# One stage's instruction order and weight loads, and the queues of stores and gates, in a three-part transformer block

## The chip, the cores and the metric

The kernel runs on one core of a Trainium2 chip. The core has a matrix engine (TensorE, PE in the profile, with its weight load as PEld), VectorE (DVE), ScalarE (ACT), GpSimd (POOL) and SyncE (SP); each runs its own instructions in order, and semaphores join them. SP and POOL issue the transfers here. The metric is the device time of one execution in microseconds (us), the median of several.

## The reference, cut to what matters

```python
def reference(q, k, v, g_norm, moe_*, moe2_*):       # q, k, v: [8, 8, 576, 64]
    kv = einsum('bhsd,bhse->bhde', k, v)
    o = einsum('bhsd,bhde->bhse', q, kv)
    x = (o / rms(o) * g_norm) as [4608, 512]          # attention without softmax
    expert = argmax(norm(x) @ norm(expert_emb).T / tau)   # 8 experts, top 1
    x = gate * (relu(x @ w1[expert]) @ w2[expert])    # 512 -> 1024 -> 512
    h = x @ w_in                                      # 512 -> 2048
    return (h * cos(h)) @ w_out                       # 2048 -> 512
```

All data are float32, but `w_in` and `w_out`, which come as 64-bit numbers.

## The kernel before

It has three stages. Products are made to float32 precision out of three matmuls each: every operand is split into a high part (a copy by ScalarE into the matmul's format) and a low part (the difference, by VectorE), and high x high, high x low and low x high are added in PSUM (`PASS`, L229).

**Attention** (0 to about 185 us): the products with k, v and q, the norm, the logits, and a scatter of the tokens to their experts' rows.

**Experts** (about 185 to 625 us): 16 chunks of 304 tokens, in turns `g` of one eighth of a chunk (130 turns). A turn runs `layer1` and, two turns later, `layer2` of a slice, splits a piece of expert weights that SP loaded some three turns earlier (`load_piece`, L125, `split_piece`), and does a slice of the next chunk's gate (`gate_x`, L161). A gate is stored to and loaded back from a small table (L207 to 212), by POOL for chunks 1 to 10, else by SP (`BY_POOL`, L74); the same constant says who stores a chunk's `perm` rows and its result in `yT` (`store_y`, L259). Beside this the weights of the last stage are converted: from turn 16 on (`2 * OPEN`, L1097) two or three times a turn the generator `conv` is advanced, which reads 64-bit weights by POOL, rounds them on VectorE, forms Strassen-like sums of the blocks and stores seven 256 KB units for each eighth of `w_in` (`ws`) and of `w_out` (`wo`) by POOL (`prepare`, L411, L438). The tile `WAB[0]` that these stores read is later the ring of streamed weights.

**Last stage** (from about 625 us): nine blocks of 512 tokens (`NB`), each in eight steps of 256 hidden columns: 72 steps `i`, then two more for what lags. Both matrix products use the Winograd form of Strassen's method: seven products in place of eight. Step `i` does three things at once. TensorE makes the seven hidden products of step `i` ("h" units, named A11, S1, S2, S4, S3, A12, A22 after their weights) and the six or seven output products of step `i - 2` ("o" units a11, a22, s2, a12, s3, s1, and on odd steps `t`, two units long); `units` (L448) gives their order. A unit has six matmuls of 128x128 by 256 columns. VectorE and ScalarE finish the hidden values of step `i` (two halves, `h1` and `h0`: the sums of the products, then turns of the angle, `parts`, the cosine, and the product with it) and form sums and high and low parts of step `i - 1`.

The hidden products go to two PSUM banks, `ha` and `hb`, one buffer each. Each is read before the next unit may write it: `one` (ScalarE copies `ha` after A11), `five` (copies `hb` after S1), `two` (copies `ha` after S2), then VectorE adds `two` and `hb` (`h1`, first half), `five` and `ha` (`h1`, second half), `one` and `hb` (`h0`, first half), and ScalarE copies `ha` (`h0`, second half). A next step's A11 needs that last copy. `t` is put into `hb` too. The order on each engine is the order of the text in `step` (L1265): the cosine of the half left from the step before and its product on VectorE come first (L1293), then `one` (L1316), the sums, `five`, the highs; at the end come turns, `parts` of the second half (L1380 to 1382). The next block's tokens are split by `tokens_of` (L344), a generator that is advanced once after each step (L1404).

SP loads weights in the order of use into a ring of `RS` = 9 slots of 256 KB (`slot`, `feed`, L461 to 474): each unit that used a slot calls `feed` for the unit nine further. Of the output weights, four units of each eighth are kept in SBUF (`KEPT`, 32 quarters of 256 KB): `keep` loads four of them at a time, for two eighths ahead of step 0 and for one ahead of each of steps 1 to 6 (L1389 to 1392). The final sums of a block stand at the start of the second step after it (`after`), behind sums in the step before that (`done`); POOL scatters the rows out.

## Time and profile before

| | us |
|---|---|
| median of 3 runs | 1478.63 (1478.52 to 1481.57) |
| the profiled execution | 1477.85 |
| its span, first to last instruction | 1476.4 |
| attention stage | 0 to 185 |
| experts stage | 185 to 624.7 |
| last stage, steps 0 to 7 | 624.7 to 720.4 |
| last stage, steps 8 to 71 | 720.4 to 1450.7 |
| rest | 1450.7 to 1476.4 |

Durations and starts come from the profiled execution; the median is that of other executions, 0.8 us apart here. A matmul's end is modelled, and matmuls overlap, so the distance of two starts tells more than a duration. The lists of waits name the engine and line that waited, and what ended the wait.

### The profile page before, as it was taken

The page shows a single profiled execution, that of the slowest core. Times are in us where ns is not written, and L with a number is a line of the kernel's source. Part 1 is how long each engine was busy: PE and PEld are TensorE (multiplying, and loading weights), DVE is VectorE, ACT ScalarE, POOL GpSimd, SP SyncE. Part 2 cuts the span into 40 slices and gives each one's busy share as a digit, 9 for nine tenths or more (in the row PEclk, how much of TensorE's full clock was granted, in tenths as well). Part 3 has the DMA queues.
Part 4 walks back from the last instruction along what each step waited for, and adds up shares of the span by engine and source line. Part 5 has one row for each costly group of instructions (what it writes and reads, how often), then busy time and mean ns, then how long its engine had stood idle before and what let it go on. Part 6 is the DMA issues. An engine that isn't in the chain of part 4 may idle for free. (4 is left out here: it accounts for less than half of the span.)

```text
span 1476.4 us, 30084 instructions
## 1 busy us (share of the span) xinstructions
PE 1343.0 (91%) x10825; PEld 1302.5 (88%) x10825; DVE 1124.5 (76%) x2551; ACT 780.8 (53%) x1601; POOL 229.6 (16%) x407
## 2 busy tenths in 40 slices
PE   7997999999999999978998989989899898998995
PEld 6876999899999999968988989889898898988995
DVE  2568869988988987557777878778687787777875
ACT  4567355554555454345555555555555555555552
POOL 1242323333433331000010100101001010010101
PEclk9999999999999999989999999999999999999998
DMA  9998587977988874499777878778677787886782
GB/s 267 307 314 251 179 208 233 287 240 238 265 255 231 265 250 127 131 331 329 244 273 226 272 239 259 265 231 281 221 260 263 228 278 229 254 275 220 254 263 100
DMA packets 233795, 363.28 MB, mean 246 GB/s; under 512 B 26604, under 2 KB 113424, under 8 KB 232424
## 3 DMA queue, kind: packets, MB, share of 16 engines
q1 hardware_dynamic: 209368, 277.20, 60.3%
q0 software_dynamic: 24256, 84.06, 17.6%
q8 instruction: 89, 1.46, 0.4%
q14 instruction: 66, 0.54, 0.1%
q10 hardware_dynamic: 16, 0.02, 0.0%
HBM read 302.24 MB, written 58.96 MB: 245 GB/s over the span
## 5 line engine op out<-in xcount | busy, mean ns | idle before, releaser
L254 PE MATMUL y<-h,ring 128*128 128x304 f32 x1536 | 237.6, 304 | 13.6 <-DVE yo L262 12.9
L237 PE MATMUL hps<-xT,ring 128*128 128x304 f32 x1536 | 244.6, 309 | 3.1 <-DVE xT L226 2.9
L254 PEld LDWEIGHTS y<-h,ring 128*128 128x128 f32 x1536 | 221.4, 189 | 15.9 <-issue 12.8
L237 PEld LDWEIGHTS hps<-xT,ring 128*128 128x128 f32 x1536 | 222.4, 191 | 5.4 <-DVE xT L226 4.3
L1162 ACT ACTIVATE u<-u,half_pi 128x512 f32<-128x512 f32 x144 | 103.6, 720 | 157.6 <-DVE u L1159 157.6
L1253 POOL DMA_INDIRECT out<-o_sb,perm_i x36 | 39.1, 1086 | 857.8 <-DVE o_sb L1226 518.6
L1245 DVE TENSOR_TENSOR h<-h,u 128x512 f32<-128x512 f32 x144 | 99.3, 690 | 85.5 <-ACT u L1162 84.7
L1156 ACT ACTIVATE u<-h 128x512 int32<-128x512 f32 x144 | 91.0, 632 | 133.1 <-DVE lo L1229 129.6
L1186 PE MATMUL ha<-ring,wa 128*128 128x256 f32 x738 | 115.7, 294 | 24.8 <-ACT one L1223 17.7
L1186 PEld LDWEIGHTS ha<-ring,wa 128*128 128x128 f32 x738 | 99.0, 196 | 32.3 <-ACT one L1223 23.6
L1196 PE MATMUL o_a<-ring,hi 128*128 128x256 f32 x640 | 122.8, 284 | 0.0
L1159 DVE SCALAR_TENSOR_TENSOR u<-h,u 128x512 f32<-128x512 f32 x144 | 98.8, 686 | 23.6 <-ACT u L1156 23.6
L1186 PE MATMUL ha<-xb,wa 128*128 128x256 f32 x600 | 92.6, 290 | 24.9 <-ACT one L1223 21.2
L1186 PEld LDWEIGHTS ha<-xb,wa 128*128 128x128 f32 x600 | 79.0, 191 | 31.8 <-ACT one L1223 26.9
L1196 PEld LDWEIGHTS o_a<-ring,hi 128*128 128x128 f32 x640 | 99.5, 192 | 0.0
L1229 DVE TENSOR_TENSOR lo<-u,hi 128x512 fp32r<-128x512 f32 x144 | 98.4, 684 | 0.0
L141 DVE TENSOR_TENSOR ring<-raw,ring 128x1024 fp32r<-128x1024 f32 x72 | 87.7, 1218 | 12.5 <-ACT ring L140 12.3
L1196 PE MATMUL o_s<-wa,hi 128*128 128x256 f32 x456 | 86.9, 282 | 4.8 <-DMA wa<-wo 4.8
L1196 PE MATMUL o_a<-ring,lo 128*128 128x256 f32 x320 | 90.3, 282 | 0.6 <-DVE lo L1229 0.6
L1223 ACT ACTIVATE hi<-u 128x512 fp32r<-128x512 f32 x144 | 88.7, 628 | 3.5 <-DVE u L1229 0.2
L243 ACT ACTIVATE h<-hps 128x304 fp32r<-128x304 f32 x128 | 53.2, 416 | 70.1 <-PE hps L237 68.7
L244 DVE SCALAR_TENSOR_TENSOR h<-hps,h 128x304 fp32r<-128x304 f32 x128 | 59.7, 466 | 35.4 <-ACT h L243 35.1
(271 smaller groups left out, 3083.7 us busy)
## 6 DMA issues: line engine op xcount, KB each, us to landing
wa<-ws SPq DMA_DIRECT2D x390, 256.0 KB
wa<-wo SPq DMA_DIRECT2D x170, 256.0 KB
raw<-in_moe_w SPq DMA_DIRECT2D x144, 256.0 KB
ring<-ws SPq DMA_DIRECT2D x114, 256.0 KB
ring<-wo SPq DMA_DIRECT2D x78, 256.0 KB
ws<-wa POOLq DMA_DIRECT2D x56, 256.0 KB, 5.3
wo<-wa POOLq DMA_DIRECT2D x56, 256.0 KB, 4.9
xr<-xs POOLq DMA_DIRECT2D x16, 627.0 KB, 7.6
```

The costliest lines, as they stand in the source:

```text
L141: nc.vector.tensor_tensor(out=w[:, 1], in0=raw, in1=w[:, 0].bitcast(F32), op=ALU.subtract)
L237: nc.tensor.matmul(out=p[:, 0:CH], lhsT=w[:, a, k * 128:(k + 1) * 128], rhs=c["xT"][b_][k], start=(n == 0), stop=(n == 11),)
L244: V.scalar_tensor_tensor(out=lo, in0=p[:, 0:CH], scalar=0.0, in1=hi.bitcast(F32), op0=ALU.max, op1=ALU.subtract)
L254: nc.tensor.matmul(out=c["y"][d][:, 0:CH], lhsT=w[:, a, 512 + d * 128:512 + (d + 1) * 128], rhs=h[b_], start=(f == 0 and i == 0), stop=(f ...
L1156: nc.scalar.activation(out=n, in_=p, func=ACTF.Copy, scale=TURN, bias=0.25)
L1159: V.scalar_tensor_tensor(out=u, in0=p, scalar=TURN, in1=n, op0=ALU.mult, op1=ALU.subtract)
L1162: nc.scalar.activation(out=u, in_=u, func=ACTF.Sin, scale=2 * math.pi, bias=half_pi)
L1186: nc.tensor.matmul(out=out, lhsT=w[:, a, k * 128:(k + 1) * 128], rhs=x[xi][:, b_, k * 256:(k + 1) * 256], start=(start and n == 0), stop=( ...
L1196: nc.tensor.matmul(out=o[:, th * 256:th * 256 + 256], lhsT=G[j, name][a][:, th * 128:th * 128 + 128], rhs=w[:, b_, 0:256], start=(start an ...
L1223: nc.scalar.activation(out=out, in_=in_, func=ACTF.Copy)
L1229: V.tensor_tensor(out=out, in0=x, in1=y, op=ALU.subtract)
L1245: V.tensor_tensor(out=Y[j, t], in0=Y[j, t], in1=Y["u", t], op=ALU.mult)
```

## The change

- In `step`, ScalarE's `one` and `five` come ahead of the cosine of the half left over, with its `parts` now first on VectorE (they stood last in the step before); the sums and highs are dealt out anew between the reads of the banks; `h0`'s first add and `parts` come ahead of the last low. `t` moves ahead of `s3`. Sums of a finished block move to the step's end.
- `tokens_of` yields about twice as often, and is advanced twice inside a step: after the first high part (ScalarE's halves) and after `one` (VectorE's sums and lows).
- Kept weights: the first four quarters have a tile of their own and are loaded before the stage; the other 28 are loaded singly, one behind every second feed, at most for the next eighth but one.
- `prepare` hands the stores of `wo` to a list; SP issues one or more of them each turn, and seven ahead of the next use of their tile.
- `BY_POOL` falls from 11 to 3: gates, rows and results of chunks 3 to 10 go by SP.
- The conversion starts at turn 9 and is advanced once in a turn that splits a piece (before turn 40), else twice, three times in some.

```diff
@@ -71,7 +71,7 @@
     EARLY, EARLY_T = 2, 24
-    BY_POOL = 11
+    BY_POOL = 3
     VISITS = [(0, [0]), (1, [0, 1]), (0, [1])] + [(e, [0, 1]) for e in range(2, E)]
@@ -382,31 +380,45 @@
-        yield
+        for _ in range(4 if b else 0):
+            yield
         t1 = minus(b12, raw[0])
+        yield
         half(3, t1)
         half(0, raw[0])
-        yield
+        if b:
+            yield
         t6 = minus(raw[2], b12)
         lows()
+        yield
         half(6, t6)
-        yield
+        if b:
+            yield
         t2 = minus(raw[2], t1)
         lows()
+        yield
         half(4, t2)
         half(2, raw[2])
-        yield
+        if b:
+            yield
         t5 = minus(raw[1], t2)
         lows()
+        yield
         half(5, t5)
         half(1, raw[1])
-        yield
+        if b:
+            yield
         lows()
...
-    WA, WAB, WOUT = {}, [], {}
+    WAB, WOUT, stores = [], {}, []
+
+    def store_some(n):
+        for _ in range(min(n, len(stores))):
+            o, x = stores.pop(0)
+            nc.sync.dma_start(out=o, in_=x)
@@ -430,12 +442,16 @@
         t = WAB[0]
+        store_some(7)
         for i, n, src in ((0, 2, a[:, 0:512]), (2, 2, a[:, 512:1024]), (4, 3, o)):
...
         for u in range(7):
-            nc.gpsimd.dma_start(out=store[u], in_=t[:, u].rearrange("p a c -> p (a c)").bitcast(F32))
+            if layer:
+                stores.append((store[u], t[:, u].rearrange("p a c -> p (a c)").bitcast(F32)))
+            else:
+                nc.gpsimd.dma_start(out=store[u], in_=t[:, u].rearrange("p a c -> p (a c)").bitcast(F32))
@@ -451,7 +467,7 @@
             h(A11, B11), h(S1, T1), o("a11", W11), h(S2, T2), h(S4, B22), o("a22", W4), h(S3, T3), o("s2", V2),
-            h(A12, B21), o("a12", W21), h(A22, T4), o("s3", V3), *last, o("s1", V1),
+            h(A12, B21), o("a12", W21), h(A22, T4), *last, o("s3", V3), o("s1", V1),
         ]
@@ -472,13 +488,20 @@
         fed[0] += 1
-
-    def keep(q_):
-        WOUT[q_] = ring(WO[q_])
-        for j, w in enumerate(KEPT):
-            nc.sync.dma_start(
-                out=WOUT[q_][:, :, j * 256:j * 256 + 256].bitcast(F32), in_=wo[q_, w].rearrange("p (a c) -> p a c", a=2)
-            )
+        if fed[0] > RS and fed[0] % 2 and keeping and keeping[0][0] <= STREAM[fed[0] - RS][1] + 1:
+            keep_one()
+
+    keeping = [(q_, j) for q_ in range(8) for j in range(len(KEPT))]
+
+    def keep_one():
+        q_, j = keeping.pop(0)
+        if j == 0:
+            WOUT[q_] = ring(WO[q_ - 1]) if q_ else first_kept[0]
+        nc.sync.dma_start(
+            out=WOUT[q_][:, :, j * 256:j * 256 + 256].bitcast(F32), in_=wo[q_, KEPT[j]].rearrange("p (a c) -> p a c", a=2)
+        )
+
+    first_kept = []
@@ -1074,10 +1097,12 @@
                 cvctx.close()
-                if RS > 9:
-                    WAB.append(ctx.enter_context(tc.tile_pool(name="wb", bufs=1)).tile([128, RS - 9, 2, 256], F32R, name="wb"))
+                store_some(7)
+                first_kept.append(ctx.enter_context(tc.tile_pool(name="wb", bufs=1)).tile([128, 2, 1024], F32R, name="wb"))
                 for _ in range(RS):
                     feed()
+                for _ in KEPT:
+                    keep_one()
             if g < OPEN:
@@ -1094,8 +1119,9 @@
                 late.sort(key=lambda x: x[0])
-            if g >= 2 * OPEN:
-                for _ in range(3 if g % 4 == 0 and not splits else 2):
+            store_some(1 + len(stores) // 5)
+            if g >= START:
+                for _ in range(1 if splits and g < 5 * OPEN else 3 if g > 6 * OPEN and g % 6 == 0 and not splits else 2):
                     next(conv, None)
@@ -1282,16 +1308,16 @@
-            if after:
-                prior = b - 1
-                o1, o2 = OUT[prior]
-                add(o2[:, :, 256:512], halves(E1), halves(bank[prior, "s1"]))
-                add(o1[:, :, 256:512], halves(U2), halves(bank[prior, "s1"]))
-                out_rows(prior, 0, o1)
-                out_rows(prior, 1, o2)
+            if new:
+                xa = ps_h.tile([128, 512], F32, name="ha", tag="ha")[:, 0:256]
+                xb = ps_h.tile([128, 512], F32, name="hb", tag="hb")[:, 0:256]
+                h1, h0 = (hp_.tile([128, 512], F32, name="h", tag="h") for _ in range(2))
+                Y[i, 1], Y[i, 0] = h1, h0
+                one, five, two = (sn.tile([128, 256], F32, name=nm, tag=nm) for nm in ("one", "five", "two"))
+            else:
+                xa = xb = None
             if prev:
-                cos_of(last, 0)
-                mul_of(last, 0)
+                parts_of(last, 0)
                 r0, r1, s13, s24 = (two_of(x) for x in (Y.pop((last, 0)), Y.pop((last, 1)), Y["u", 1], Y["u", 0]))
@@ -1302,30 +1328,30 @@
                 G[last, "a22"] = (hi1[:, 0], lo1[:, 0])
-            xa = xb = None
-            if new:
-                xa = ps_h.tile([128, 512], F32, name="ha", tag="ha")[:, 0:256]
-                xb = ps_h.tile([128, 512], F32, name="hb", tag="hb")[:, 0:256]
-                h1, h0 = (hp_.tile([128, 512], F32, name="h", tag="h") for _ in range(2))
-                Y[i, 1], Y[i, 0] = h1, h0
-                one, five, two = (sn.tile([128, 256], F32, name=nm, tag=nm) for nm in ("one", "five", "two"))
+                copy(hi1[:, 0], r1[:, 1])
+                add(s13[:, 0], r1[:, 0], r1[:, 1])
+                sub(lo1[:, 0], r1[:, 1], f32(hi1[:, 0]))
+            pump()
             h(xa, True)
...
                 copy(one, xa)
-            if prev:
-                add(s13[:, 0], r1[:, 0], r1[:, 1])
-                sub(s13[:, 1], r0[:, 0], r1[:, 0])
-                sub(s24[:, 0], s13[:, 0], r0[:, 0])
-                sub(s24[:, 1], r0[:, 1], s24[:, 0])
+            if after:
+                prior = b - 1
+                o1, o2 = OUT[prior]
+                add(o2[:, :, 256:512], halves(E1), halves(bank[prior, "s1"]))
+                add(o1[:, :, 256:512], halves(U2), halves(bank[prior, "s1"]))
+                out_rows(prior, 0, o1)
+                out_rows(prior, 1, o2)
+            pump()
             if new:
...
             if prev:
-                copy(hi1[:, 0], r1[:, 1])
-                copy(hi0, r0)
-            if done:
-                copy(E1, bank[b, "a11"])
+                cosine(Y["u", 0])
+                V.tensor_tensor(out=r0, in0=r0, in1=two_of(Y["u", 0]), op=ALU.mult)
+                sub(s13[:, 1], r0[:, 0], r1[:, 0])
+                sub(s24[:, 0], s13[:, 0], r0[:, 0])
             h(xa, False)
@@ -1333,38 +1359,39 @@
             if prev:
+                sub(s24[:, 1], r0[:, 1], s24[:, 0])
+                copy(hi0, r0)
                 copy(hi13, s13)
                 copy(hi24, s24)
-                sub(lo1[:, 0], r1[:, 1], f32(hi1[:, 0]))
                 sub(lo0, r0, f32(hi0))
+            if done:
+                copy(E1, bank[b, "a11"])
             h(xa, False)
             o()
+            if prev:
+                sub(lo13, s13, f32(hi13))
             if new:
                 add(h1[:, 256:512], five, xa)
+                turns_of(i, 1)
             if done:
                 add(U2, E1, bank[b, "s2"])
-            if prev:
-                sub(lo13, s13, f32(hi13))
             if new:
...
             o()
+            if new:
+                add(h0[:, 0:256], one, xb)
+                parts_of(i, 1)
             if done:
...
                 add(OUT[b][0][:, :, 0:256], halves(E1), halves(bank[b, "a12"]))
-            if new:
-                turns_of(i, 1)
-                add(h0[:, 0:256], one, xb)
             if prev:
                 sub(lo24, s24, f32(hi24))
+            if new:
+                cos_of(i, 1)
+                mul_of(i, 1)
             h(xa, False)
-            o()
-            if done:
-                add(E1, U2, bank[b, "s3"])
-                add(OUT[b][1][:, :, 0:256], halves(E1), halves(bank[b, "a22"]))
             if new:
-                parts_of(i, 1)
-                cos_of(i, 1)
                 copy(h0[:, 256:512], xa)
@@ -1373,23 +1400,26 @@
                     add(Y["acc"], Y["acc"], t)
-                if done:
-                    add(U2, U2, Y["acc"])
             o()
+            o()
+            if done:
+                add(E1, U2, bank[b, "s3"])
+                add(OUT[b][1][:, :, 0:256], halves(E1), halves(bank[b, "a22"]))
+                add(U2, U2, Y["acc"])
             if new:
                 turns_of(i, 0)
-                mul_of(i, 1)
-                parts_of(i, 0)
             assert not todo
...
         scr = lambda: sx.tile([128, 512], F32, name="sx", tag="sx")
-        coming = None
+        coming = iter(())
+
+        def pump():
+            next(coming, None)
+
         for i in range(NS + 3):
             b, q_ = divmod(i, 8)
-            if i == 0:
-                keep(0)
-            if i < 7:
-                keep(i + 1)
+            if q_ == 0 and b + 1 < NB:
+                coming = tokens_of(b + 1, scr)
             if i < NS + 2:
@@ -1398,10 +1428,6 @@
                 out_rows(NB - 1, 1, o2)
-            if q_ == 0 and b + 1 < NB:
-                coming = tokens_of(b + 1, scr)
-            if coming:
-                next(coming, None)
             for x in range(2 * i, min(2 * i + 2, NB)):
```

Left out here: `OPEN, START = 8, 9`, the yields of `tokens_of` ahead of its first difference, and `slot` without its second tile.

## Rows read from the trace of the kernel before

**Rows 1.** The page: its first line.

```profile
span 1476.4 us, 30084 instructions
```

**Rows 2.** Table of stretches: us, busy (instructions) of each engine; PEclk, DMA, GB/s.

```profile
185.00:624.69 439.69, 422.22 (x3068) 416.82 (x3067) 370.98 (x876) 218.04 (x427) 133.70 (x251) 0.99 0.77 228
624.69:720.40 95.71, 78.83 (x591) 76.93 (x590) 62.64 (x126) 48.65 (x99) 0.00 (x0) 0.93 0.91 307
720.40:1450.67 730.27, 673.41 (x5378) 655.01 (x5377) 567.07 (x1118) 406.89 (x833) 35.16 (x32) 0.99 0.77 252
```

**Rows 3.** Waits of PE from 624 us on: total us, times, longest.

```profile
PE ha L1186 <- ACT one L1223: 50.2, 39, 1.8
...
PE ha L1186 <- DMA ring<-ws: 4.1, 1, 4.1
```

**Rows 4.** Timeline of step 22, from 880.12: start us, us, instruction, idle time before.

```profile
880.12 0.88 PE L1186 MATMUL ha<-ring,wa 128*128 128x256 f32 x6
...
880.84 0.88 PE L1186 MATMUL hb<-ring,wa 128*128 128x256 f32 x6
...
882.14 0.63 ACT L377 ACTIVATE xb<-sx 128x512 fp32r<-128x512 f32 x1 [2.80 <-DVE sx L371]
...
883.20 0.71 ACT L1162 ACTIVATE u<-u,half_pi 128x512 f32<-128x512 f32 x1
883.81 0.36 ACT L1223 ACTIVATE one<-ha 128x256 f32<-128x256 f32 x1
...
884.22 0.97 PE L1186 MATMUL ha<-ring,ring 128*128 128x256 f32 x6 [1.79 <-ACT one L1223]
```

**Rows 5.** Timeline of the stage's first step, units A11 and S1.

```profile
624.69 0.87 PE L1186 MATMUL ha<-ring,ring 128*128 128x256 f32 x6
625.40 0.88 PE L1186 MATMUL hb<-ring,ring 128*128 128x256 f32 x6
625.60 0.39 ACT L1223 ACTIVATE one<-ha 128x256 f32<-128x256 f32 x1 [4.55 <-PE ha L1186]
```

**Rows 6.** Table of stretches: steps 19 and 20, and steps 16 to 23.

```profile
845.48:856.56 11.08, 11.07 (x91) 10.87 (x91) 7.83 (x16) 6.33 (x14) 0.00 (x0) 1.00 1.01 371
856.56:867.91 11.35, 9.61 (x81) 9.32 (x79) 7.65 (x16) 6.90 (x16) 0.00 (x0) 1.00 0.60 183
...
812.46:904.22 91.76, 83.22 (x674) 80.85 (x673) 71.67 (x142) 51.34 (x105) 4.30 (x4) 1.00 0.77 252
```

**Rows 7.** Groups of ScalarE, 720 to 1450: busy us, mean ns | idle before.

```profile
L1162 ACT ACTIVATE u<-u,half_pi 128x512 f32<-128x512 f32 x128 | 92.1, 720 | 142.8 <-DVE u L1159 142.8
```

**Rows 8.** Timeline of VectorE from 906.73: the product with the cosine, two differences.

```profile
906.73 0.68 DVE L1245 TENSOR_TENSOR h<-h,u 128x512 f32<-128x512 f32 x1
907.33 0.42 DVE L1226 TENSOR_TENSOR u<-h 128x256 f32<-128x256 f32 x1
907.66 0.42 DVE L1229 TENSOR_TENSOR u<-h 128x256 f32<-128x256 f32 x1
```

**Rows 9.** Table of stretches: one at half clock, and step 1.

```profile
952.35:955.76 3.41, 3.41 (x18) 3.41 (x17) 2.15 (x6) 1.52 (x4) 0.00 (x0) 0.50 0.57 151
...
631.41:644.49 13.08, 7.02 (x43) 6.64 (x43) 7.42 (x16) 5.79 (x13) 0.00 (x0) 0.87 1.01 353
```

**Rows 10.** Waits of the experts stage, 185 to 625: us, times, longest (SPq: SP's queue).

```profile
POOL wo L438 <- DVE wa L341: 46.7, 12, 13.6
POOL gates L208 <- DVE gt L201: 29.9, 6, 12.1
...
DVE yo L262 <- DMA gate<-gates: 4.0, 2, 2.3
DVE start L487 <- POOL starti L486: 2.1, 1, 2.1
...
PE y L254 <- DVE yo L262: 12.9, 8, 3.1
...
SPq L208 <- DVE gt L201: 52.2, 5, 20.4
```

More of the change, by code (lines that the diff above doesn't have):

```diff
@@ L92, in tile_kernel @@
     NC = len(chunks)
-    OPEN = 8
+    OPEN, START = 8, 9
     use, at = [], 0
@@ L365, in tokens_of @@
         yield
-        if b > 1:
-            yield
         def minus(x, y):
@@ L383, in lows @@
             later.clear()
+        for _ in range(4 if b else 0):
+            yield
+        t1 = minus(b12, raw[0])
         yield
-        t1 = minus(b12, raw[0])
         half(3, t1)
         half(0, raw[0])
-        yield
+        if b:
+            yield
         t6 = minus(raw[2], b12)
         lows()
+        yield
         half(6, t6)
-        yield
+        if b:
+            yield
         t2 = minus(raw[2], t1)
         lows()
+        yield
         half(4, t2)
         half(2, raw[2])
-        yield
+        if b:
+            yield
         t5 = minus(raw[1], t2)
         lows()
+        yield
         half(5, t5)
         half(1, raw[1])
-        yield
+        if b:
+            yield
         lows()
@@ L464, in slot @@
             return XAT[3][:, n, 512:1024].rearrange("p (a c) -> p a c", a=2)
-        return WAB[0][:, n - 2] if n < 9 else WAB[1][:, n - 9]
+        return WAB[0][:, n - 2]
     def feed():
```

## The prediction

> **What bounds the kernel now.** The profiled execution has a span of 1476.4 us [rows 1] and a time of 1477.85, 0.8 under the median 1478.63. I first cut the span into its stages with the table of stretches [rows 2], then asked in the longest stage who makes TensorE wait [rows 3], then laid one step of it out in time [rows 4]. The reader should see this in turn. The first 72 steps of the last stage (from 624.69 on) take 826 us. From step 8 to 72 it has 730.27 us, 5378 matmul records, TensorE's mean clock at 0.99, VectorE 567 us busy and ScalarE 407 [rows 2]: no engine but TensorE is near full, yet TensorE waits. What it waits for is nearly one thing: the copy `one` on ScalarE, 50.2 us in 39 waits [rows 3]. A wait counts from the modelled end of the matmul before, so the loss is larger than that sum; I take it from starts.
>
> A unit of six matmuls starts 0.72 us after the one before (880.12 to 880.84 [rows 4]) or 0.71 (624.69 to 625.40 [rows 5]): I take 0.716. An even step has 13 units (7 hidden, 6 out), an odd one 15 (the `t` product is two more): 9.31 and 10.74 us, 80.2 for eight steps. The block at 812.46 took 91.76; its odd step of 11.08 shows that the floor is within reach, the even one of 11.35 loses 2 us [rows 6]. Steps 8 to 72 have a floor of 8 x 80.2 = 641.6, so 88.7 of 730.3 us are lost there.
>
> The reason stands in the step at 880.12 [rows 4]. In the stage's first step `one` starts 0.9 us after its unit did, 0.2 after the next [rows 5]; that is when a bank can be read. Here ScalarE, which runs in order, has token halves (from 882.14) and the cosine of the step before (883.20) ahead of `one`; `one` starts at 883.81, and the unit S2, due at 882.27, starts at 884.22. The cosine is itself late: over steps 8 to 72 ScalarE waits 142.8 us ahead of it, all for VectorE's `parts` [rows 7].
>
> **The last stage, by parts.** (1) `one` and `five` go ahead of the cosine, `parts` of the half before goes to the step's first place on VectorE, and the add that frees `hb` goes ahead of three lows. I lay a step in this order on each engine with durations from rows: 0.68 for 512 columns on VectorE (the next starts 0.60 later), 0.42 for 256 (0.33 later) [rows 8], 0.72 a cosine [rows 7], 0.36 a short copy, 0.63 a long one [rows 4]. Times count from the step's first matmul. ScalarE: `one` 0.95 to 1.32, `five` 1.66 to 2.03, cosine to 2.7, `two` 3.1 to 3.5, three highs with their waits to 5.65, turns 6.6 to 7.2, second cosine 8.0 to 8.7, last copy to 8.95. VectorE: parts to 0.69, one add, one low, token work if any to 2.6, product with the cosine to 3.4, differences, the add that frees `hb` by 4.64, two lows, the add that frees `ha` by 6.5, the next by 7.1, parts to 7.9, low, product to 9.4. TensorE needs `one` at 2.15, `five` at 2.87, `two` at 4.30, `hb` at 5.73, `ha` at 7.16 and the last copy at 9.31: all in time, with the least slack, 0.35 us, at the last. So plain even steps run at 9.31 and odd ones at 10.74.
>
> What is late next: the two steps after a block's end, where VectorE has extra work. Three sums of 512 columns left from the step before push `parts` to 1.56 instead of 0; two final sums and one token difference add 1.8 ahead of the product. The product starts at 4.64 instead of 2.7, `hb` is freed at 6.58 (0.9 late), `ha` 0.45 late, the last copy 0.3: 1.6 us in all; the next step still loses 0.45, and one step with two token lows 0.15. That is 2.2 us a block, 17 over eight blocks: 641.6 + 17 = 659. The bounds of this term are 0 (all cover holds) and, if every step's slack is used up by small delays that I did not lay out, about 0.5 us a step, 32 us.
>
> (2) The clock. A stretch of 3.41 us at 0.50, the 1.2 GHz level, follows waits of TensorE: at 952.35 [rows 9]; there are ten in the last stage, six of them from step 8 on. Each costs 1.7 us. With most waits gone I keep two of the six: 659 + 3 = 662, against 730.3: 68 us gained.
>
> (3) Steps 0 to 7. They took 95.71 us at 307 GB/s [rows 2], 29.4 MB, against 2 x 5.0 + 3 x (9.31 + 10.74) = 70.2 us of matmuls. In step 1 the transfers ran at 353 GB/s with a busy share of 1.01 [rows 9]: full. Eight kept loads are queued there ahead of the stream, and TensorE waits 4.1 us for `ring<-ws` [rows 3]. Loaded one by one, a kept quarter stands behind every second stream load, and the first four (1.05 MB) come before the stage. The queue on SP gets 28 more issues between the feeds; a feed waits only for the unit that frees its slot, so nothing is queued behind a long wait. The bytes stay: 28.3 MB at 353 GB/s is 80 us, the floor here, above the matmuls. I take 82 with the slow first two steps, a gain of 14 (bounds 6, if the rate is that of before with fewer stalls, and 20).
> The Trainium skill ("DMA: Bandwidth & Descriptors", Specifications) gives some 358 GB/s as a core's HBM limit, by which 28.3 MB would take 79 us. The trace shows 371 GB/s for one step of 11.08 us [rows 6], a little over it; by that the term would be 76.
>
> (4) From step 8 on the stream stays 252 GB/s x 730.27 us = 184 MB, and 662 us ask 278 GB/s of it, under 353; nine slots ride over the bursts of token loads and final rows. At nothing. If this cover fails, see the rivals. The four token loads of a block reach SP one step's feeds earlier, into a queue that is under its limit. The `t` product's new place and the two pumps a step change the order alone; they are in the layout. The 26 us at the end stay.
>
> **The stage before (185 to 624.69).** Gates, rows and stores of `yT` of chunks 3 to 10 (8 x 7 issues) and 56 stores of output weights leave POOL's queue for SP's. On POOL the gates wait 29.9 us for VectorE and the weights' stores 46.7, with the loads of raw weights and the index work queued behind [rows 10]. VectorE's `yo` waits 4.0 us for a gate and 2.1 for POOL's index work, and TensorE waits 12.9 us, 8 times, for `yo` [rows 10]. Gates that come in time and an unblocked POOL take off about 6 us; the two stretches at half clock in this stage, each after such a wait, another 3.4. The other waits are VectorE's own backlog, which the earlier start of the conversion (turn 9, not 16) thins by 7 turns in 108. Against it: SP now waits for `gt` (52.2 us in 5 such waits [rows 10]) and for the stores' sources, ahead of piece loads that have three turns of lead, 3 x 439.69 / 130 = 10 us. I take 1.5 us of harm: 8 us gained, with bounds 16 gained and 8 lost.
> The Trainium skill (same page, Issuing engines are not separate DMA queues) says that all issuing engines share the same 16 DMA engines, and that another issuer saves only issue time, usually small. By it this term would be nothing; the trace bears it out for bytes, but what I count is a wait in an in-order queue.
>
> **Sum.** 68 + 14 + 8 = 90 us off: 1477.85 - 90 = 1387.9, and 0.8 for the median: 1388.6, say 1388.
>
> **Rivals.** *The new order makes a wait in place of the old.* ScalarE's first copy of a step, `hi1`, stands ahead of `one` and waits for the second product, which ends 0.1 us into the step in my layout; each us that VectorE slips beyond 0.8 there reaches TensorE. At half a us a step, 32 us: 1420. For it: VectorE is 78% busy now and would be at 86%. Against: most of its idle time now is waiting, and eight steps hold only 71.7 us of its work [rows 6] for 82.
> *The stream can't follow.* If 184 MB came at 265 GB/s, the rest of the stage would take 694 instead of 662: 1420. For it: 278 GB/s was needed in no long stretch after step 8. Against: 371 GB/s in one step and 353 at full share in another [rows 6, 9].
> *Nothing in the stage before*, the rule on issuing engines: 1477.85 - 82 + 0.8 = 1396.6.
> *Slower: SP's queue holds up the piece loads.* With eight more gates on SP, each may wait 10.4 us (the mean) to 20.4 [rows 10]. A piece load has 10 us of lead less 3.5 of transfer, so what exceeds 6.5 us stops ScalarE's split and with it TensorE: at the mean 8 x 3.9 = 31 us, at the longest 8 x 13.9 = 111, which beats all gains: 1478 + 111 - 82 = 1507. It decides from 6.5 + 82 / 8 = 16.8 us a gate. Against: five gates already go by SP, and no row shows the split waiting for a piece.
> *It doesn't do what it says*, `one` still waits as now: only 14 + 8 come, 1457.
>
> **How the numbers follow.** Forecast 0.62 (1372 to 1402 by its own bounds), nothing in the stage before 0.15, new wait 0.08, stream 0.07, `one` still late 0.04, SP slower 0.04. Range: down to 1372, up to 1425, which takes in both cases of 1420. 0.2% (3 us) is about what a measurement of this kernel tells from no change. Faster 0.96, same 0.01, slower 0.03.
>
> **What would show it.** In the changed profile: the wait `ha` for `one` under 10 us; plain even steps 9.3 to 9.5 us apart, blocks of 82 to 84; steps 0 to 7 in 80 to 85; fewer stretches at 0.50; a rate near 278 GB/s; POOL's gates and weights' stores gone, `yo`'s gate wait gone. I am wrong if TensorE's waits move to `hb` or to transfers by more than 20 us, or if ScalarE's split waits for pieces.

## The result and the profile after

The changed kernel takes 1379.35 us (median, 1379.04 to 1383.31) against 1480.1 for the kernel before: ratio 0.9325, 95% interval 0.9303 to 0.9347. The forecast was 1388, range 1372 to 1425. The profiled execution took 1379.59 us. First its span, for [rows 1], then the stretches that answer to [rows 2] and [rows 6]: experts stage, steps 0 to 7, steps 8 to 71, the block of steps 16 to 23, and of it the two steps behind a block's end, 18 and 19.

```profile
span 1377.7 us, 30179 instructions
```

```profile
185.00:610.23 425.23, 419.12 (x3083) 417.20 (x3083) 369.78 (x878) 218.62 (x427) 75.95 (x139) 1.00 0.80 239
610.23:695.75 85.52, 76.96 (x592) 75.61 (x590) 64.31 (x131) 49.83 (x100) 0.00 (x0) 0.90 0.94 315
695.75:1352.40 656.65, 649.79 (x5378) 642.62 (x5377) 562.87 (x1119) 419.89 (x833) 35.28 (x32) 1.00 0.86 282
778.69:860.62 81.93, 81.20 (x674) 80.37 (x673) 71.11 (x143) 52.89 (x105) 4.24 (x4) 1.00 0.86 283
798.70:809.41 10.71, 9.98 (x80) 9.36 (x78) 10.02 (x21) 5.31 (x11) 4.24 (x4) 1.00 0.85 278
809.41:820.56 11.15, 11.15 (x90) 10.94 (x91) 9.54 (x20) 8.15 (x17) 0.00 (x0) 1.00 0.87 300
```

Against [rows 2], 14.5 us went in the experts stage, 10.2 in steps 0 to 7, 73.6 in steps 8 to 71 and 0.4 at the end: 98.7, the difference of the spans. In steps 8 to 71 VectorE does as much as before (563 us busy against 567) in 73.6 us less. TensorE's four longest waits from 610 us on, for [rows 3]: `one` is gone.

```profile
PE hb L1212 <- DVE h L1252: 5.2, 8, 1.9
PE ha L1212 <- DMA ring<-ws: 3.9, 1, 3.9
PE ha L1212 <- ACT h L1249: 2.7, 2, 1.5
PE ha L1212 <- DVE h L1252: 1.5, 8, 0.2
```

Step 22 in time, for [rows 4]: ScalarE's token halves start 0.39 us ahead of the step, `one` starts 0.91 into it and waits for TensorE alone, the cosine comes after `five`, and the unit S2 is on time at 842.74.

```profile
840.21 0.62 ACT L375 ACTIVATE xb<-sx 128x512 fp32r<-128x512 f32 x1
840.60 0.88 PE L1212 MATMUL ha<-ring,wa 128*128 128x256 f32 x6
841.51 0.38 ACT L1249 ACTIVATE one<-ha 128x256 f32<-128x256 f32 x1 [0.17 <-PE ha L1212]
842.51 0.71 ACT L1188 ACTIVATE u<-u,half_pi 128x512 f32<-128x512 f32 x1
842.74 0.88 PE L1212 MATMUL ha<-ring,ring 128*128 128x256 f32 x6
```

The cosines' wait for VectorE, 142.8 us in [rows 7], is 49.2 in the first row below (groups of ScalarE, steps 8 to 71). The other two rows are the only stretches at the 1.2 GHz level from the stage's start to the end of step 71: both in its first steps, none from step 8 on, where before had six like [rows 9].

```profile
L1188 ACT ACTIVATE u<-u,half_pi 128x512 f32<-128x512 f32 x128 | 92.2, 721 | 50.2 <-DVE u L1185 49.2
```

```profile
617.20:630.85 13.65, 8.49 (x39) 7.93 (x38) 6.21 (x14) 5.35 (x11) 0.00 (x0) 0.50 0.87 277
634.25:637.70 3.45, 3.45 (x19) 3.45 (x18) 2.45 (x5) 1.72 (x5) 0.00 (x0) 0.51 1.03 372
```

### The profile page after: what moved, and what is told of

The parts are those of the page before. It is cut to its first block, busy times and chain, and to the rows that moved or that the text cites. A ratio compares the mean times of both kernels' runs of the same rounds, so it can differ in the third digit from the quotient of the medians.

```text
span 1377.7 us, 30179 instructions
## 1 busy us (share of the span) xinstructions
PE 1315.7 (95%) x10825; PEld 1291.3 (94%) x10825; DVE 1118.0 (81%) x2551; ACT 795.2 (58%) x1601; POOL 172.8 (13%) x295
## 5 line engine op out<-in xcount | busy, mean ns | idle before, releaser
L237 PE MATMUL hps<-xT,ring 128*128 128x304 f32 x1536 | 241.1, 306 | 5.7 <-DVE h L244 3.0
L237 PEld LDWEIGHTS hps<-xT,ring 128*128 128x128 f32 x1536 | 219.5, 189 | 7.2 <-DVE h L244 3.7
L1212 PE MATMUL ha<-ring,wa 128*128 128x256 f32 x738 | 111.5, 288 | 3.5 <-ACT h L1249 2.7
L1222 PE MATMUL o_a<-ring,hi 128*128 128x256 f32 x568 | 107.8, 282 | 0.0
L1212 PE MATMUL ha<-xb,wa 128*128 128x256 f32 x600 | 88.6, 283 | 0.7 <-DVE h L1252 0.5
L1249 ACT ACTIVATE hi<-h 128x256 fp32r<-128x256 f32 (+1 forms) x144 | 74.8, 519 | 25.1 <-DVE h L1352 25.1
L1352 DVE TENSOR_TENSOR h<-h,u 128x512 f32<-128x512 f32 x72 | 49.6, 689 | 48.2 <-ACT u L1188 48.0
L1222 PEld LDWEIGHTS o_a<-ring,hi 128*128 128x128 f32 x568 | 87.1, 189 | 0.0
L1212 PE MATMUL hb<-ring,wa 128*128 128x256 f32 x558 | 83.7, 287 | 2.8 <-DVE h L1252 2.8
```

Of the source, the lines that this page charges most:

```text
L237: nc.tensor.matmul(out=p[:, 0:CH], lhsT=w[:, a, k * 128:(k + 1) * 128], rhs=c["xT"][b_][k], start=(n == 0), stop=(n == 11),)
L1212: nc.tensor.matmul(out=out, lhsT=w[:, a, k * 128:(k + 1) * 128], rhs=x[xi][:, b_, k * 256:(k + 1) * 256], start=(start and n == 0), stop=( ...
L1222: nc.tensor.matmul(out=o[:, th * 256:th * 256 + 256], lhsT=G[j, name][a][:, th * 128:th * 128 + 128], rhs=w[:, b_, 0:256], start=(start an ...
L1249: nc.scalar.activation(out=out, in_=in_, func=ACTF.Copy)
L1352: V.tensor_tensor(out=r0, in0=r0, in1=two_of(Y["u", 0]), op=ALU.mult)
```

## The experiments

They ran on other chips than the two measurements above; the kernel before took 1488.6 to 1489.7 us in the median there, the stages ahead of the last being up to 15 us longer. So each ratio is taken within its own group of runs, and the working goes by stretches of the profiles. The old order took 730.3, 733.3, 733.7, 735.4 and 735.7 us for steps 8 to 71 in five kernels, the new one 655.1 to 656.7 in four: that is the scatter of such a stretch. Steps 0 to 7 with the old order and kept loads in batches scatter more: 93.6, 94.2, 95.7, 99.0 and 101.8 us in five kernels.

**What holds up the last stage from step 8 on.** The forecast named ScalarE's order (theory 1 in the expectations); the rival is VectorE's (theory 2).

*`one` alone* (on the kernel before):

```
-                cos_of(last, 0)
-                mul_of(last, 0)
...
                 copy(one, xa)
+                copy(five, xb)
             if prev:
+                cosine(Y["u", 0])
+                V.tensor_tensor(out=r0, in0=r0, in1=two_of(Y["u", 0]), op=ALU.mult)
...
-            if new:
-                copy(five, xb)
```

> The kernel before with one thing moved: ScalarE's copies `one` and `five` stand ahead of the cosine at the start of each step of the last stage; VectorE's order, the token work and the loads are left. Theory 1 (the prediction's: ScalarE has the cosine ahead of `one`, and that is why PE waits): the 91 us of PE waits for `one` go and the stage gives back most of the 68 us that steps 8 to 71 lost by the forecast, so 50 to 70 us less than before. Theory 2 (VectorE's queue sets the pace: it stands idle while both cosines run, and ScalarE's token halves wait for VectorE's differences; `one` is only the first read to be late): the waits move to later reads of the same banks (`two`, the copy of the second half, the h sums), and laying the queues' rows end to end gives 2 to 5 us less.

1467.21 us, ratio 0.9868 (0.9818 to 0.9919). Steps 8 to 71, and what TensorE waits for there:

```profile
719.86:1436.64 716.78, 671.37 (x5379) 647.42 (x5377) 559.02 (x1118) 413.35 (x833) 36.13 (x32) 1.00 0.79 256
```

```profile
PE ha L1186 <- ACT one L1223: 27.2, 28, 1.2
PE ha L1186 <- ACT h L1223: 9.8, 10, 1.1
PE ha L1186 <- ACT two L1223: 4.8, 19, 0.4
```

13.5 us of the 73.6, or up to 19 by the scatter of the old order: neither theory's number. `one` is still waited for 28 times, with the cosine behind it; in the kernel before it was 36 times and 45.5 us from step 8 on, and the 91 us that the expectation names stand in no view.

*The order as a whole* (the kernel before with the new step, units and token work; kept loads in batches):

```
+            if q_ == 0 and b + 1 < NB:
+                coming = tokens_of(b + 1, scr)
             if i == 0:
                 keep(0)
...
```

> The kernel before with the whole new order of the last stage (units, reads, VectorE's and ScalarE's orders, token work in halves), kept weights still loaded in batches of four and the experts stage as before. Both theories: steps 8 to 71 take 657 +- 5 us instead of 730, no half-clock stretch after step 8, steps 0 to 7 stay at 90 to 96 us; 1478.6 - 75 = 1404 +- 8 us. If much more than 75 us goes, the order also made steps 0 to 7 shorter; if much less, the kept loads or the experts stage carry part of what was put down to the order.

1401.78 us, ratio 0.9397 (0.9361 to 0.9432). Steps 0 to 7, then 8 to 71:

```profile
639.88:731.05 91.17, 76.82 (x592) 74.69 (x590) 63.97 (x129) 50.06 (x100) 0.00 (x0) 0.94 0.95 322
731.05:1386.13 655.08, 649.25 (x5378) 642.36 (x5377) 562.96 (x1119) 419.90 (x833) 34.98 (x32) 1.00 0.87 281
```

The whole gain from step 8 on is the order's; loads and experts stage have no part in it.

*The cosine ahead of `one` again* (on the changed kernel):

```
                 parts_of(last, 0)
+                cosine(Y["u", 0])
...
-                cosine(Y["u", 0])
                 V.tensor_tensor(out=r0, in0=r0, in1=two_of(Y["u", 0]), op=ALU.mult)
```

> The changed kernel with one thing undone: the cosine of the second half stands ahead of `one` and `five` on ScalarE again. Theory 1 (the place of `one` is the cause): waits for `one` come back in every step, 40 to 55 us more in steps 8 to 71 (656.7 to some 700). Theory 2 (VectorE's queue is the cause, and `one` late only because ScalarE's queue was held up by it): the cosine no longer waits for VectorE, since its operand is written at the very start of the step, and costs its own 0.62 us ahead of a read that has a slack of about that size: 0 to 5 us more.

1420.73 us, ratio 0.9534 (0.9512 to 0.9557). Steps 0 to 7 and 8 to 71; TensorE's largest wait; step 22:

```profile
617.27:702.25 84.98, 75.30 (x591) 72.62 (x590) 64.76 (x131) 49.17 (x99) 0.00 (x0) 0.98 0.94 316
702.25:1393.81 691.56, 657.11 (x5378) 644.18 (x5377) 568.99 (x1119) 415.06 (x833) 35.28 (x32) 1.00 0.82 268
```

```profile
PE ha L1212 <- ACT one L1249: 30.4, 37, 1.4
```

```profile
856.64 0.88 PE L1212 MATMUL ha<-ring,wa 128*128 128x256 f32 x6
856.74 0.72 ACT L1188 ACTIVATE u<-u,half_pi 128x512 f32<-128x512 f32 x1 [1.14 <-DVE u L1185]
857.67 0.61 ACT L375 ACTIVATE xb<-sx 128x512 fp32r<-128x512 f32 x1
858.71 0.36 ACT L1249 ACTIVATE one<-ha 128x256 f32<-128x256 f32 x1
859.13 0.98 PE L1212 MATMUL ha<-ring,ring 128*128 128x256 f32 x6 [0.17 <-ACT one L1249]
```

34.9 us more. Theory 2, which gave at most 5, falls for this place; theory 1's 40 to 55 is missed from below. ScalarE waits 1.14 us for VectorE's `parts`, then `hi1` and two token halves follow, and `one` starts 2.07 us into the step instead of 0.91; S2, due at 858.79, starts 0.34 late.

*VectorE's order undone in two places* (on the changed kernel):

```
-                add(s13[:, 0], r1[:, 0], r1[:, 1])
-                sub(lo1[:, 0], r1[:, 1], f32(hi1[:, 0]))
...
                 V.tensor_tensor(out=r0, in0=r0, in1=two_of(Y["u", 0]), op=ALU.mult)
+                add(s13[:, 0], r1[:, 0], r1[:, 1])
+                sub(lo1[:, 0], r1[:, 1], f32(hi1[:, 0]))
...
                 add(h0[:, 0:256], one, xb)
-                parts_of(i, 1)
...
                 sub(lo24, s24, f32(hi24))
             if new:
+                parts_of(i, 1)
                 cos_of(i, 1)
```

> The changed kernel with VectorE's order undone in two places: lo24 stands ahead of the parts of the first half again (so the first cosine starts later), and the first sum and lo1 stand behind the product with the second cosine (so VectorE has nothing to do while that cosine runs). ScalarE's order, the place of `one` too, is left. Theory 1: `one` is still ahead of the cosine, 0 to 5 us more. Theory 2: VectorE idles for both cosines, 0.3 to 0.6 us more in plain steps and more behind a block's end; 12 to 25 us more in steps 8 to 71.

1400.8 us, ratio 0.9398 (0.9374 to 0.9423). Steps 8 to 71:

```profile
698.94:1374.62 675.68, 659.91 (x5378) 644.96 (x5377) 550.14 (x1118) 425.87 (x833) 37.74 (x32) 1.00 0.84 274
```

19.0 us more, inside theory 2's range, with `one` ahead of the cosine all the time. So there are two causes.

*The token work undone* (on the changed kernel: one `pump` behind each step, the generator of before):

```
...
-            pump()
             h(xa, True)
...
+            if q_ == 0 and b + 1 < NB:
+                coming = tokens_of(b + 1, scr)
+            pump()
```

> The changed kernel with the token work undone: in batches behind a step's end as before, ScalarE's halves right behind the VectorE differences that they need. Theory 1: the halves no longer stand ahead of `one`... they stand behind it, so 0 to 3 us either way. Theory 2: VectorE, no longer late, answers the halves at once, so that alone it costs little too, 0 to 5 us; what counts is that it comes on top of a late VectorE. If it costs over 10 us, the token halves are a cause of their own, beside the order.

1377.24 us, ratio 0.9256 (0.9227 to 0.9285). Steps 8 to 71, and steps 18 and 19:

```profile
695.24:1347.48 652.24, 647.70 (x5379) 641.94 (x5378) 564.41 (x1119) 420.38 (x833) 37.94 (x32) 1.00 0.87 284
796.77:806.86 10.09, 9.86 (x80) 9.37 (x78) 9.40 (x20) 5.30 (x11) 4.71 (x4) 1.00 0.91 308
806.86:817.68 10.82, 10.82 (x90) 10.82 (x91) 8.52 (x18) 7.26 (x15) 0.00 (x0) 1.00 0.97 346
```

4.4 us less: this part of the change costs a little. The two steps behind a block's end take 20.91 us together, 21.86 in the changed kernel; step 23 gives part of it back (11.34 us, 10.73 in the changed kernel).

**What sets steps 0 to 7.** Four edits.

*Kept weights one by one* (on the kernel before: `keep` replaced by `keep_one`, as in the diff):

> The kernel before with the kept weights alone loaded one by one among the feeds (the first four at the end of the experts stage). If steps 0 to 7 were set by bytes and by batches of kept loads standing ahead of feeds: 8 to 14 us less in steps 0 to 7 (95.7 to 82 .. 88). If they were set by the same engine queues as the later steps, and by the late feeds of steps 0 and 1: 0 to 4 us less. Steps 8 to 71 unchanged (730 +- 3).

1479.87 us, ratio 0.9946 (0.9912 to 0.998). Steps 0 to 7:

```profile
636.71:726.06 89.35, 76.91 (x591) 74.18 (x590) 63.28 (x128) 48.44 (x99) 0.00 (x0) 0.96 0.91 302
```

6.4 us less than [rows 2], short of the theory of bytes and batches (8 to 14) and over its rival's (0 to 4); the order alone gave 4.5 (91.17, above). Together that is 10.9, near the change's 10.2; but by the scatter of 93.6 to 101.8 us each of the two is known to some 8 us only, so the sum decides little.

*Block 1's token loads behind step 0's feeds* (on the changed kernel):

```
...
-            if q_ == 0 and b + 1 < NB:
+            if i == (1 if b == 0 else 8 * b) and b + 1 < NB:
```

> The changed kernel with block 1's token loads put on SP's queue one step later, behind step 0's feeds (its arithmetic stays where it is). If SP's queue is what makes steps 0 and 1 long (the token loads wait there for the last stores of the experts stage and the feeds stand behind them): the wait of 3.9 us for a stream slot in step 1 goes, steps 0 and 1 take 19 to 20 us instead of 23.4, and perhaps the half-clock stretch at 617 us shrinks; steps 0 to 7 some 81 us instead of 85.5. If bytes are the limit (the forecast's floor of 80 us): the same bytes have to land, steps 0 to 7 stay at 85 +- 1 us, the wait only moves to a later step.

Why it was tried shows in SP's queue in the changed kernel (timeline): the last stores of `yT`, then token loads (`yT` to `xb`, `sx`) that wait for them, then the first feed.

```profile
614.37 2.09 SPq L270 DMA_DIRECT2D yT<-yo  x4
617.34 0.42 SPq L356 DMA_DIRECT2D xb<-yT  x1
...
621.34 0.93 SPq L487 DMA_DIRECT2D ring<-ws  x2
```

1380.04 us, ratio 0.9265 (0.9239 to 0.929). Steps 0 to 3 and their eight together:

```profile
610.89:620.29 9.40, 5.46 (x44) 5.05 (x42) 3.59 (x9) 2.79 (x7) 0.00 (x0) 1.00 0.52 120
620.29:629.28 8.99, 6.02 (x43) 5.26 (x43) 7.34 (x16) 6.01 (x13) 0.00 (x0) 1.00 0.93 320
629.28:642.49 13.21, 11.59 (x79) 11.06 (x79) 8.52 (x17) 6.55 (x14) 0.00 (x0) 0.87 1.01 349
642.49:654.20 11.71, 10.96 (x92) 10.79 (x91) 9.32 (x19) 7.63 (x17) 0.00 (x0) 1.00 0.92 309
610.89:695.97 85.08, 75.19 (x592) 72.60 (x590) 64.52 (x131) 49.90 (x100) 0.00 (x0) 0.98 0.94 319
```

Step 1 takes 8.99 us instead of 14.70, the long half-clock stretch is gone, and the other steps give nearly all of it back, steps 2 and 3 the most (24.9 instead of 21.6): 85.1 against 85.5. As the theory of bytes says, the wait only moved.

*Half the bytes of the kept weights* (on the changed kernel):

```
-            out=WOUT[q_][:, :, j * 256:j * 256 + 256].bitcast(F32), in_=wo[q_, KEPT[j]].rearrange("p (a c) -> p a c", a=2)
+            out=WOUT[q_][:, 0, j * 256:j * 256 + 256].bitcast(F32), in_=wo[q_, KEPT[j], :, 0:256]
...
```

In the products the high part then stands in for the low one, so this kernel leaves out part of the result.

> The changed kernel with half of each kept weight's bytes left out (the low part of the four kept weights isn't loaded, and the high part stands in for it in their products, so that part of the result is left out; the matmuls are as many as before). In steps 0 to 7 this takes 28 times 0.13 MB = 3.7 MB from SP's queue of about 27 MB. If bytes set these steps, as the forecast had it (and as it looks now that four kernels with different queues all take 85 to 86.5 us there): 3.7 MB at 330 to 360 GB/s = 10 to 11 us less, 74 to 77 us. If the engines' orders or the late first feeds set them: 85 +- 1 us as before. Steps 8 to 71 unchanged.

1379.0 us, ratio 0.9274 (0.9234 to 0.9313). Steps 0 to 7 (steps 8 to 71 took 656.73 us, as ever):

```profile
615.63:692.64 77.01, 72.21 (x591) 70.80 (x590) 63.47 (x129) 49.92 (x100) 0.00 (x0) 1.00 0.93 311
```

8.5 us less, 77.0, though its chip took longer ahead of the stage. With the two orders that cost 34.9 and 19.0 us later, steps 0 to 7 took 85.0 (above) and 85.9 us: there the loads weigh most, not these orders. The whole old order with the same single loads took 89.35, so by that one run the order has a share of some 4 us. Step 0 was 2.0 us shorter here than in the changed kernel, so 6.5 to 8.5 are the halved loads'; packets fell with the bytes (15,666 against 18,769), and the run can't part the two.

**The experts stage,** taken apart: all its parts, the gates alone (`BY_POOL = 3`), and gates with stores (`store_some`), all on the kernel before.

```
-    BY_POOL = 11
+    BY_POOL = 3
...
+            store_some(1 + len(stores) // 5)
-            if g >= 2 * OPEN:
-                for _ in range(3 if g % 4 == 0 and not splits else 2):
+            if g >= START:
+                for _ in range(1 if splits and g < 5 * OPEN else 3 if g > 6 * OPEN and g % 6 == 0 and not splits else 2):
```

> The kernel before with the experts-stage parts alone: gates of chunks 3 to 10 by SP, output weights' stores by SP dealt out over the loop, conversion begun seven groups earlier and paced otherwise. If these parts alone make the stage's 14.5 us: 1464 +- 2 us, experts stage 425 us, and the last stage as before. If part of the gain comes from what the last stage's new order asks of this stage's end: 1467 to 1472.

> The kernel before with one part of the experts-stage change alone: the gates, position rows and scaled outputs of chunks 3 to 10 go by SP instead of POOL. If POOL's in-order queue, where the gate's two moves stand behind weight stores that wait for VectorE, is what made VectorE and PE wait: the 12.9 us of PE waits for the scaled outputs go, 8 to 14 us less in the experts stage (439.7 to 426 .. 432). If SP's queue holds them up as long as POOL's did, or the conversion's order is the cause: 436 to 441.

> The same with the output weights' stores by SP too, dealt out over the loop; only the conversion's pacing is left as before. If the stores matter beside the gates: 3 to 6 us less again in the experts stage than with the gates alone. If not, within 2 us of the run with the gates alone, and what is then missing to 425 us is the pacing's.

All parts: 1472.29 us, ratio 0.9873 (0.9838 to 0.9909); gates alone 1489.72, 1.0012 (0.9985 to 1.0039); gates and stores 1484.96, 0.9975 (0.9948 to 1.0001). Chunks 3 to 10, from first matmul to first matmul, in the kernel before, with the gates, with gates and stores, with all parts:

```profile
232.57:474.70 242.13, 230.47 (x1666) 227.24 (x1665) 216.69 (x493) 125.27 (x244) 91.36 (x169) 0.99 0.86 258
```

```profile
235.43:473.06 237.63, 229.16 (x1667) 224.46 (x1666) 216.33 (x493) 125.02 (x244) 65.97 (x119) 1.00 0.88 260
```

```profile
235.97:473.57 237.60, 229.18 (x1666) 224.47 (x1665) 216.32 (x493) 125.00 (x244) 54.67 (x98) 1.00 0.89 257
```

```profile
240.76:464.71 223.95, 223.95 (x1666) 223.92 (x1665) 203.94 (x470) 120.17 (x234) 52.40 (x91) 1.00 0.86 244
```

The expectation for all parts, 1464 us, missed by 8. It was counted from 1478.6 us; against its own group's 1488.6 the run is 16.3 us shorter. In its profile the experts stage was as short as forecast (the last stage began at 610.52), but steps 0 to 7 took 101.8 us, the longest of the five kernels with the old order and batches, and steps 8 to 71 took 3 us more than before. In chunks 3 to 10 the gates give 4.5 us, the stores nothing, the pacing (with the earlier start) 13.7 on top of both: with it VectorE has 12.4 us less to do in these chunks, and TensorE no idle time in them (224 us busy of 224). The 4.5 us are no more than the scatter: with the old stage these chunks took 241.9 to 247.1 us in four kernels. Nor do they come through: with the gates alone the last stage began at 623.08 us against 624.69, where 426 to 432 us for the stage, and so 611 to 617, were expected, and the time was the same. Chunk 2, which takes the conversion's new start, is 5 us longer in the changed kernel (33.3 against 28.2). The expectation that the gates alone would end the waits for `yo`, 12.9 us in [rows 10], fell: with the gates alone they are 9.3 us, with the stores too 12.2. The pacing was not run by itself.

**A version that goes on** (on the changed kernel): three sums behind a block's end leave VectorE.

```
-                add(o2[:, :, 256:512], halves(E1), halves(bank[prior, "s1"]))
-                add(o1[:, :, 256:512], halves(U2), halves(bank[prior, "s1"]))
...
+                copy(o2, halves(bank[prior, "s1"]))
+                nc.gpsimd.tensor_tensor(out=o1, in0=halves(U2), in1=o2, op=ALU.add)
+                nc.gpsimd.tensor_tensor(out=o2, in0=halves(E1), in1=o2, op=ALU.add)
...
-                add(U2, U2, Y["acc"])
+                (nc.gpsimd if new else V).tensor_tensor(out=U2, in0=U2, in1=Y["acc"], op=ALU.add)
```

> A version that goes on: the changed kernel with three of the sums behind a block's end taken off VectorE. ScalarE copies the bank s1 to where its sum is to lie, and GpSimd makes the two sums with it and adds the kept product's sum to U2. The two steps behind a block's end lost 1.4 and 0.4 us each in the changed kernel, eight times: if VectorE's queue is what sets them, they come to 9.3 and 10.8 .. 11.0, 10 to 14 us less in steps 8 to 71 (656.7 to 643 .. 647). If GpSimd's sums hold VectorE up (rows of GpSimd: 209 ns for 8 elements, 250 for 24, by which 512 take an estimated 1.5 us), or PE then waits for the bank: 652 to 660.

1376.03 us, ratio 0.9246 (0.9214 to 0.9277); 653.57 for steps 8 to 71, 3.1 less. Steps 18 and 19, and rows of GpSimd and VectorE about 808 us:

```profile
800.37:810.14 9.77, 9.49 (x81) 9.29 (x79) 9.27 (x17) 5.78 (x11) 4.14 (x3) 1.00 0.80 252
810.14:822.02 11.88, 11.26 (x90) 10.95 (x91) 10.29 (x21) 8.12 (x17) 4.93 (x5) 1.00 0.91 294
```

```profile
807.21 1.30 POOL L1364 TENSOR_TENSOR o_sb<-u,o_sb 128x512 f32<-128x512 f32 x1 [5.23 <-ACT o_sb L1249]
808.59 1.61 POOL L1365 TENSOR_TENSOR o_sb<-e,o_sb 128x512 f32<-128x512 f32 x1
807.31 0.41 DVE L1252 TENSOR_TENSOR h<-one,hb 128x256 f32<-128x256 f32 x1
808.15 0.90 DVE L1185 SCALAR_TENSOR_TENSOR u<-h,u 128x512 f32<-128x512 f32 x1 [0.43 <-ACT u L1182]
808.98 1.77 DVE L1255 TENSOR_TENSOR lo<-u,hi 128x512 fp32r<-128x512 f32 x1
```

The same low in the changed kernel:

```profile
808.25 0.68 DVE L1255 TENSOR_TENSOR lo<-u,hi 128x512 fp32r<-128x512 f32 x1
```

Step 18 gains 0.94 of the 1.4 us, step 19 loses 0.73: beside GpSimd's second sum VectorE's low takes 1.77 us instead of 0.68, the parts of the next half come later, and with them everything up to the next `one`. The rival in the expectation decides. Its median and that of the token run are below the changed kernel's 1379.35, from other chips; by the stretches both gain 3 to 4 us, near what a whole run can tell.

## Why the forecast held, and where its terms were off

The terms were 68 + 14 + 8 = 90 us; measured, from span to span, were 73.6 + 10.2 + 14.5 + 0.4. So +5.6, -3.8, +6.5 and +0.4 make the 8.7 that the time lay lower.

**(1) The order.** Right in mechanism and, as a layout of the whole, in size: 659 us without the clock, measured 656.65. Plain steps take 9.3 and 10.74 us; the two steps behind a block's end lose as named, a block of 81.93 standing 1.7 us over 80.2 instead of 2.2. The part that failed is the paragraph that begins "The reason": it puts the loss down to what ScalarE has ahead of `one`, names VectorE's lateness beside it, and can't tell them apart. `one` moved by itself brings 13.5 us, its place taken back at the end costs 34.9, VectorE's two swaps 19.0 and the token work -4.4. Neither theory's range held for `one` in either direction. Taking `one`, the swaps and the token work back one at a time makes 49.5 of 73.6: the other 24 are moves not singled out (units, sums at a block's end, the product's place) or are shared among the causes. How they divide stays open. A read that stands right behind a long wait of its own engine isn't late by its place alone.

**(2) The clock.** Two stretches of half clock were kept from step 8 on, at 3 us for both; there is none. At the forecast's 1.7 us for each this is about half of the 5.6; but the price isn't borne out. With the old order the kernel before has six such stretches from step 8 on and took 730.3 us, the four others have two or three and took 733.3 to 735.7. In steps 0 to 7 the half clock showed no cost beyond 0.4 us: with 0.90 as the mean they took 85.5 us, with 0.98 in the run with later token loads 85.1.

**(3) Steps 0 to 7.** The bytes are the main limit, as the step said; the run with half the kept bytes bears it out. Mis-sized were both factors: 26.9 MB (315 GB/s x 85.52 us) instead of 28.3, and 315 GB/s instead of 353. The first step explains most of the rate: 8.75 us at 102 GB/s is 0.9 MB, the other 26.0 MB in 76.8 us make 339. What failed is "a feed waits only for the unit that frees its slot, so nothing is queued behind a long wait": SP's feeds stood behind the last stores of `yT`, which wait for the last gate, and behind block 1's token loads, which wait for these stores, until 621.34. In the run with later token loads the first feed came at 617.88 and nothing was won; whether the stores on another queue would help was not tried.

**(4) The stream** followed at 282 GB/s, and the one wait for a transfer that is longer than 0.9 us lies in step 1.

**(5) The experts stage.** 14.5 us instead of 8, and mostly from another edit than the one that I priced. I took 6 us for gates and POOL, 3.4 for the clock, and priced the earlier, more even conversion at nothing beside a remark that it thins VectorE's backlog. In chunks 3 to 10 the gates gave 4.5, no more than the scatter, the stores 0.0 and the pacing 13.7. Of the two stretches at half clock one came back elsewhere: chunk 2 of the changed kernel has 3.41 us at 0.50, from 211.00 on. The rule of the Trainium skill ("DMA: Bandwidth & Descriptors", Issuing engines are not separate DMA queues) did well on the two edits that it bears on: both together left the start of the last stage at 625.68 us, against 624.69 before. The rival that gave the whole stage nothing fell by the pacing.

**The rivals.** SP does wait for `gt` more, 94.1 us in 12 waits with 12.3 as the longest, but under the 16.8 a gate at which that rival would decide, and ScalarE's splits wait 3.4 us in all for pieces. The 3.5 us that this rival gives a piece's transfer stand in no row: by the trace of the kernel before, 27 piece loads with no other issue of SP within 5 us took 3.1 to 8.9 us from issue to last packet, 5.2 in the median, by which it would decide from an estimated 15.1. The new wait, `hi1` ahead of `one`, stays out: among TensorE's waits above none is for `one`.

## What to carry to other kernels

Where an engine is late on a read, look at what the instruction ahead of it in that queue waits for: moving the read alone gave 13.5 us here, the new order of both engines as a whole 73.6. Before costing an order, ask whether the stretch is bound by bytes: in steps 0 to 7 two orders that differ by 35 us later cost the same to 0.6 us. Work that only has to be done by some time is worth spreading at an even pace from the first moment on; in chunks 3 to 10 of the experts stage that brought 13.7 us on top of the shorter queue, which by itself left the time as it was.

## What the hardware showed

GpSimd's sums slow some of VectorE's instructions and leave others alone. In the last run 24 VectorE instructions from 700 to 1350 us took over 0.8 us, none in the changed kernel; all have two SBUF inputs and lie beside one of GpSimd's sums (about 0.90, 1.28 and 1.77 us instead of 0.69), 15.1 us too much in all. Sums with one input in PSUM, beside the same instructions of GpSimd, took as long as ever, 0.41 us for 256 columns and 0.69 for 512. So the layout that gave 10 to 14 us for that version lacked this cost. The Trainium skill ("SBUF — State Buffer", Who interferes with whom) says of SBUF's ports: "A DVE instruction with two SBUF inputs contends with a GpSimd instruction that reads SBUF". The trace agrees.
